# FNet mixing gated by a squared-ReLU layer, one core: a chunk's P and Q written out in two halves, and the side work of VectorE on earlier steps

## The chip, the cores and the metric

The kernel runs on one core of a Trainium2 chip. The metric is the device time of one execution in microseconds (us); lower is better. Several executions are timed and their median is compared.

## The reference, cut to what matters

```python
xn = _layernorm(x)                                    # x: 2048 x 512, over the last axis
a = einsum("bsd,ed->bse", xn, dft_hid_re)             # DFT along the hidden axis
b = einsum("bsd,ed->bse", xn, dft_hid_im)
s = einsum("ts,bse->bte", dft_seq_re, a) - einsum("ts,bse->bte", dft_seq_im, b)
h = einsum("bsd,df->bsf", xn, w1) + b1                # F = 1792
h = where(h > 0, h, 0); h = h * h
g = einsum("bsf,fd->bsd", h, w2) + b2
return x + s * silu(g)
```

All data are float32.

## The kernel before, in words

**Arithmetic.** Every float32 operand of TensorE is split into a high part, rounded by ScalarE (`split_hi`, line 136), and the rest, subtracted by VectorE (`split_lo`, line 139). Each product is three matmuls: high by high, high by low, low by high. Most products of 2 x 2 blocks go by a scheme of seven products instead of eight (`PRODUCTS`). It needs sums of blocks on both sides, which VectorE makes before the split (`sums_a_steps`, `sums_b_steps`), and sums of the seven results (`closing_of`, `combine`).

**Stages.** First come the layer norm and, with it, the products of sequence chunk 0 (`products`, line 399, with 512 columns). The two sequence transforms of xn, called P and Q, are made for eight chunks `c` of 256 rows. Chunk 0 uses plain products. Chunk 1 takes four of its eight inner steps as plain products (`MIXED`, `plain_step`) and four by the seven products; while the mixed steps run, VectorE makes the sums over xn that the scheme needs on its stationary side. Those are eight operations on 128x1024 in two groups of four inner blocks (`side[0]` and `side[1]`, made by `sums`, line 273), and after them one split for each of the eight inner blocks (`split_sums`, tile `xc`). Chunks 2 to 7 are all in the scheme: eight steps `(c, j)` of 42 matmuls (`mm`, line 388). Then follow the y units (`YUnit`, `r_A` to `r_D`, line 799), which apply the hidden transform to P and Q; the h units, which use w1; and the output products with w2 (`outer`, line 905).

**A step of a chunk.** In step n the code issues the 42 matmuls; then the sums of the DFT operand of step n+2 (`step_sums`, tile `u`, lines 300 to 303); the split of step n+1 (`step_split`: ScalarE `g<-u`, then VectorE `g<-u,g`); the load of the operand of step n+4 (`step_load`, three buffers `u`); one or two of the sums that close the chunk before (`closing`, tile `c`, made from PSUM and from copies called `left`); and last whatever the table `EARLY` names for that step. Each engine takes its instructions in this written order. There are two `g` buffers, so ScalarE can split step n+1 only once TensorE is done with step n-1.

**The closing of a chunk.** In the last step of a chunk `some(closing, 2)` starts it: ScalarE copies product 1 into tile `c`, and VectorE adds products 2 and 6. The other five sums (six for chunk 1) are spread by the tables `LATER` and `LATER_1` over steps 0 to 4 (0 to 5) of the next chunk. All chunks use one buffer, tagged `e`, for tile `c`. Its content, 1024 KB, goes to DRAM tile `pqd` in one DMA on SyncE's queue, issued at j = 5 (`max(LATER_1)`, line 660). The next chunk's first copy into tile `c` has to wait until that DMA has landed. Chunk 7 is closed after the last step, among the first y work (line 966).

**Side jobs.** `EARLY` names jobs by a letter and a number; each mention runs one piece of the job. `d0` to `d3` and `v0`, `v1`, `v6` are the weights' jobs (wd and w1): a load of the raw weight (line 438), the first sum, the other two sums, the split and DMA of three blocks, the split and DMA of four (line 451). They share two buffers tagged `pq00` and `pq01`, and `p0` to `p3` load the results back for the y units (tile `wdp`, line 499). `y0`, `y1`, `y2` are the operands of the first y units (`y_early`): a load from `pqd`, all three sums (lines 310 to 314), two splits (tile `yg`).

**SyncE's queue.** All loads of `u`, the raw weights, `wdp`, `yr` and `yraw`, and the stores to `pqd`, `wdd` and `w1d` are issued by SyncE in written order. A DMA that waits holds those behind it.

**The first y unit.** It takes product 1 (`r_A`), product 7 (`r_D`), product 6 (`r_B`), 2 (`r_A`), 5 (`r_B`), 4 (`r_C`), 3 (`r_B`). Before product 6 ScalarE must copy minus `r_A` into `r_B`; before product 3 VectorE must have read `r_B` (`c22`, line 809).

Of the kernel before, what the change touches and what calls it, by code (L numbers as in the profile page):

```python
# [34 lines left out]


EARLY = {
# [8 lines left out]
}  # L46
LATER = {0: 1, 1: 1, 2: 1, 3: 1, 4: 1}
LATER_1 = {0: 1, 1: 1, 2: 1, 3: 1, 4: 1, 5: 1}


Y_SIDE = (
# [73 lines left out]
C21, C11, C22, C12 = range(4)  # L125
# [5 lines left out]
def fnet_gated_kernel(ctx, tc, x, xt, ct, wd, w1, w2, b1, b2, out):  # L131
    nc = tc.nc
    ctx.enter_context(tc.manual_schedule(engines=None))

    def split_hi(hi, lo, src):
        nc.scalar.activation(hi, src, AF.Copy)  # L136

    def split_lo(hi, lo, src):
        nc.vector.tensor_tensor(lo, src, hi.bitcast(F32), op=ALU.subtract)  # L139

    def split(*parts):
        split_hi(*parts)
        split_lo(*parts)
# [15 lines left out]
    PQD = [dram.tile([P, 2, 4, 256], F32, name=f"pqd{c}") for c in range(NC)]  # L159
# [6 lines left out]
    def bank(tag, name):  # L166

        return acc.tile([P, 512], F32, tag=tag, name=name)
# [4 lines left out]
    def operand_buf(tag, name, step, shape=(2, 7, 256)):  # L173

        first = START.get(tag, 0)
        skip = (step - first) % 4 * LANE
        size = shape[0] * shape[1] * shape[2]
        room = ROOM.get(tag, 0)
        flat = buf(tag, [P, size + (room or skip)], name, F32R)
        a, b, c = shape  # L180
        return flat[:, skip:skip + size].rearrange("p (a b c) -> p a b c", a=a, b=b, c=c)
# [94 lines left out]
    def split_sums(j):  # L276
        s = xn32[j].rearrange("p h (b n) -> p (h b) n", b=2)
        split(XC[j][:, S2:S1 + 1, HI, :], XC[j][:, S2:S1 + 1, LO, :], s)
# [9 lines left out]
    def plain_parts(c, j, hs=slice(0, 2)):  # L288
        if (c, j) not in part:
            part[c, j] = operand_buf("g" + "ab"[j % 2], f"g{c}_{j}", 0 if c or j == NJ - 1 else 3 if j in TURNED else 1, (2, 4, CW))  # L290
        g, r = part[c, j], raw[c, j]
        s = slice(2 * hs.start, 2 * hs.stop)
        return g[:, HI, s], g[:, LO, s], r[:, s]

    def sums_b(t, r):
        list(sums_b_steps(t, r))
# [8 lines left out]
    def sums_a(*operands):  # L305
        list(sums_a_steps(*operands))

    def sums_a_steps(t, a21, a11_a22, a11, a12, turned=False):

        nc.vector.tensor_tensor(t[:, 0:2], a21.to_broadcast([P, 2, 256]), a11_a22, op=ALU.subtract)  # L310
        yield
        if turned:
            nc.vector.tensor_tensor(t[:, 2], a11, t[:, 1], op=ALU.subtract)
            nc.vector.tensor_tensor(t[:, 3], a12, t[:, 2], op=ALU.subtract)  # L314
        else:
            nc.vector.tensor_tensor(t[:, 2], t[:, 1], a11, op=ALU.subtract)
            nc.vector.tensor_tensor(t[:, 3], t[:, 2], a12, op=ALU.add)  # L317

    def sums_rows(t, r, turned=False):

        sums_a(t, r[:, C12:C12 + 1], r[:, C11:C22 + 1], r[:, C11], r[:, C21], turned)

    def sums_w1_steps(t, r):
        return sums_a_steps(t, r[:, 0:1], r[:, 1:4:2], r[:, 1], r[:, 2], True)
# [10 lines left out]
    def step_sums(n):  # L335
        if n < len(steps):
            u = raw[steps[n]]
            sums_b(u[:, 4:8], u)
# [71 lines left out]
    def plain_step(j):  # L410

        g = part.pop((1, j))
        for k, pairs_ in ((2, ((A11, 1), (A12, 3))), (4, ((A21, 1), (A22, 3))), (3, ((A11, 0), (A12, 2))),
                          (Z, ((A21, 0), (A22, 2)))):
            if k not in ms:
                ms[k] = bank("ba" if k == Z else banks(1)[k], f"m{k}_1")
            for i, (a, q) in enumerate(pairs_):
                mm(ms[k], XC[j][:, a], lambda b_: g[:, b_, q], j == MIXED[0] and not i, k == Z and j == MIXED[-1] and i == 1)
# [6 lines left out]
    def go(*names):  # L425


        for v in names:
            if v[0] == "h" and int(v[1:]) >= NTC * NP:
                continue  # L430
            if v not in making:
                making[v] = makers[v[0]](int(v[1:]))
            next(making[v])
# [46 lines left out]
    def y_early(n):  # L480

        k = n // 2
        r = buf(f"pq{k}0", [P, 4, 256], f"yr{n}")
        load_pq(n, r)
        yield
        t = buf(f"pq{k}1", [P, 4, 256], f"yt{n}")
        sums_rows(t, r, True)
        yield
        g = yop[n] = operand_buf(Y_HOME[n // 2 % 3][n % 2], f"yg{n}", 1 if n % 6 else 3)
        split(g[:, HI, 4:7], g[:, LO, 4:7], r[:, 0:3])  # L490
        yield
        split(g[:, HI, 0:4], g[:, LO, 0:4], t)
        yield
# [55 lines left out]
    side = sums(0), sums(1)  # L549
# [51 lines left out]
    def some(steps_, n):  # L601
        for _ in range(n):
            next(steps_)

    for i, j in enumerate(MIXED):
        if i == 0:
            some(side[0], 2)
            split(*plain_parts(1, MIXED[1]))
            split_sums(0)
            for k in range(ND):  # L610
                plain_out(k)
            for k in range(2):
                nc.sync.dma_start(PQD[0][:, k].rearrange("p k n -> p (k n)"), plain[k])
            some(side[1], 1)
        elif i == 1:
            split_sums(1)
            split(*plain_parts(1, MIXED[2]))
            some(side[1], 1)
            split_sums(2)
            go("d0")  # L620
        elif i == 2:
            split_sums(3)
            some(side[1], 1)
            split(*plain_parts(1, MIXED[3]))
            step_sums(0)
            go("d0", "d0")
        else:
            step_sums(1)
            some(side[1], 1)
            step_split(0)  # L630
            split_sums(4)
            split_sums(5)
        plain_step(j)
        load_c(*order[NJ + i + 4])

# [2 lines left out]
    for n, s in enumerate(steps):  # L638
        c, j = s
        if c > 1 and j == 0:  # L640
            ms = {}
        for k, tag in banks(c).items():
            if k not in ms:
                ms[k] = bank(tag, f"m{k}_{c}")
        g = part.pop(s)
        for p in FIRST if j == 0 and c > 1 else ORDER:
            a, b = PRODUCTS[p]
            mm(ms[p], XC[j][:, a], lambda b_: g[:, b_, b], j == 0 and (c > 1 or p in (1, 5, 6, 7)), s in LAST)
        step_sums(n + 2)
        step_split(n + 1)  # L650
        if n < 2:
            split_sums(6 + n)
        if n == 0:
            e = buf("e", [P, 2048], "c1")
            copy(chunk_part(e)(C22), halves(ms[Z]))
        step_load(n + 4)
        if closing:
            some(closing, (LATER_1 if c == 2 else LATER).get(j, 0))
            if j == max(LATER_1):
                nc.sync.dma_start(PQD[c - 1].rearrange("p h k n -> p (h k n)"), e)  # L660
                closing = None
        if s in LAST:
            if c > 1:
                e = buf("e", [P, 2048], f"c{c}")
            room = {}
            if c < NC - 1:
                room = buf("pq10", [P, 2, 512], f"left{c}")
                room = {7: room[:, 0], 5: room[:, 1], 3: buf("pq11", [P, 512], f"left3_{c}")}
            closing = closing_of(chunk_part(e), ms, room, c == 1)
            some(closing, 2)  # L670
        if s == (2, 4):
            nc.vector.transpose(stats_t, stats.rearrange("p m h j -> p (m h j)"))
            for q in range(4):
                nc.sync.dma_start(rows[:, q * 32:(q + 1) * 32], stats_t[q * 32:(q + 1) * 32, :])
        go(*EARLY.get(s, ()))
# [326 lines left out]
    for u in range(2, NC):  # L1002
        n = 2 * u + 2
# [41 lines left out]
    for n in range(NTC * NP):  # L1045
        unit = HUnit(n)
        first, second, later = H_SIDE.get(n, ((), (), ()))
# [39 lines left out]
    for n in range(NTC * NP):  # L1087
        c, p = divmod(n, NP)
# [37 lines left out]
        if p == NP - 1 and not last:  # L1126
            e = buf("e", [P, 4, 512], f"z{c}")
# [16 lines left out]
    e = buf("u", [P, 4, 512], f"z{c}")  # L1144
# [95 lines left out]
```

## Time and profile before

| What | Value |
|---|---|
| median of three timed runs | 676.29 us (676.1 to 677.19) |
| profiled execution: own time | 673.96 us |
| profiled execution: span | 672.1 us |
| granted TensorE clock, mean | 0.999 |
| share of the span: TensorE matmul, VectorE, ScalarE | 99%, 90%, 57% |
| DMA | 150.85 MB, mean 224 GB/s |

The profiled execution's own time stands 1.9 us above its span: that lies outside the span. PE is TensorE's matmuls and PEld its weight loads, which run beside matmuls; DVE is VectorE, ACT ScalarE, SP SyncE, SPq SyncE's queue of DMAs. In a list of waits the columns are the waiting line, the one that released it, the total in us, the number of times and the longest. In a timeline the columns are start, duration, engine, line, operation and tiles; brackets hold the engine's idle time just before and what ended it. The mean of a matmul row is its own duration; matmuls overlap.

### The profile page before, as it was taken

How to read it: one execution, taken by the hardware profiler on the slowest of the kernel's cores; microseconds unless marked ns; L12 is line 12 of the kernel's file. 1: busy time of each engine (PE TensorE's matmuls, PEld its weight loads, DVE VectorE, ACT ScalarE, POOL GpSimd, SP SyncE). 2: the span in 40 equal slices, each digit the busy share in tenths (PEclk: the TensorE clock that was granted, in tenths of full speed). 3: DMA queues.
4: the chain of work that ended last, by engine and by line, in shares of the span. 5: the costliest groups of instructions: out<-in, count | busy, mean ns of one | idle time of the engine just before them, and what ended most of it. 6: DMA issues, size and time to landing. Idle time of an engine off the chain costs nothing.

```text
span 672.1 us, 13519 instructions
## 1 busy us (share of the span) xinstructions
PE 663.7 (99%) x5605; PEld 651.5 (97%) x5605; DVE 608.0 (90%) x844; ACT 381.0 (57%) x516; POOL 8.8 (1%) x11
## 2 busy tenths in 40 slices
PE   8999999999999999999999999999999999999997
PEld 5889999999999999999899999999999999999997
DVE  7998999899989999998799988977887889999997
ACT  6855563535445454544365547788778765454451
POOL 0000000000000000000000000000000000101010
PEclk9999999999999999999999999999999999999999
DMA  8735264948659485879488668576755866677775
GB/s 284 234 105 186 87 219 145 325 138 285 238 184 352 150 282 193 280 271 319 157 298 279 201 188 299 199 262 214 267 182 196 328 241 211 179 232 194 215 204 157
DMA packets 51741, 150.85 MB, mean 224 GB/s; under 512 B 4960, under 2 KB 19552, under 8 KB 50272
## 3 DMA queue, kind: packets, MB, share of 16 engines
q1 hardware_dynamic: 43568, 129.28, 57.6%
q10 hardware_dynamic: 6208, 18.88, 7.1%
q0 software_dynamic: 1904, 1.84, 1.9%
q8 instruction: 44, 0.72, 0.4%
q14 instruction: 17, 0.14, 0.1%
HBM read 101.98 MB, written 47.99 MB: 223 GB/s over the span
## 4 chain that ended last, share of the span: by engine, by line
PE 89%; DVE 6%; DMA 2%; ACT 2%; issue 1%; SPq 0%; DVEq 0%; ACTq 0%
PE m L388 34%; PE m_o L905 15%; PE r_B L799 13%; PE r_A L799 9%; PE pq_b L399 4%; PE r_C L799 4%; PE r_D L799 4%; PE m_last L905 4%; PE pq_bb L399 1%; DMA pqd<-c 1%; DVE g L139 1%; DMA x<-in_x 1%; DVE c L373 1%; DVE xc L139 1%; DVE xn L273 1%
## 5 line engine op out<-in xcount | busy, mean ns | idle before, releaser
L388 PEld LDWEIGHTS m<-g,xc 128*128 128x128 f32 x2376 | 270.1, 188 | 0.9 <-DVE g L139 0.5
L388 PE MATMUL m<-g,xc 128*128 128x256 f32 x2376 | 270.6, 276 | 0.3 <-DVE g L139 0.3
L136 ACT ACTIVATE g<-u 128x1792 fp32r<-128x1792 f32 (+2 forms) x65 | 101.6, 1564 | 132.4 <-PE m L388 85.3
L139 DVE TENSOR_TENSOR g<-u,g 128x1792 fp32r<-128x1792 f32 (+2 forms) x66 | 120.0, 1819 | 9.1 <-ACT g L136 8.9
L905 PE MATMUL m_o<-w,g 128*128 128x256 f32 x882 | 100.5, 276 | 0.0
L905 PEld LDWEIGHTS m_o<-w,g 128*128 128x128 f32 x882 | 100.3, 188 | 0.0
L136 ACT ACTIVATE g<-hr 128x1792 fp32r<-128x1792 f32 (+2 forms) x31 | 48.2, 1565 | 40.0 <-DVE hr L317 17.8
L799 PE MATMUL r_B<-xT,w 128*128 128x256 f32 x504 | 66.5, 276 | 0.0
L799 PEld LDWEIGHTS r_B<-xT,w 128*128 128x128 f32 x504 | 61.5, 188 | 0.0
L139 DVE TENSOR_TENSOR g<-hr,g 128x1792 fp32r<-128x1792 f32 (+2 forms) x31 | 56.7, 1838 | 2.9 <-ACT g L136 2.8
L799 PE MATMUL r_A<-xT,w 128*128 128x256 f32 x336 | 43.1, 276 | 0.0
L399 PE MATMUL pq_b<-g,xc 128*128 128x512 f32 x144 | 41.2, 392 | 1.4 <-DVE small L247 1.4
L799 PEld LDWEIGHTS r_A<-xT,w 128*128 128x128 f32 x336 | 40.3, 188 | 0.2 <-DVE xT L139 0.2
L799 PE MATMUL r_B<-wdp,yg 128*128 128x256 f32 x288 | 36.0, 277 | 1.4 <-ACT r_B L146 1.2
L300 DVE TENSOR_TENSOR u<-u 128x512 f32<-128x512 f32 x52 | 35.6, 685 | 0.8 <-DMA u<-in_ct 0.7
L799 PEld LDWEIGHTS r_B<-wdp,yg 128*128 128x128 f32 x288 | 34.1, 188 | 1.8 <-ACT r_B L146 1.4
L399 PEld LDWEIGHTS pq_b<-g,xc 128*128 128x128 f32 x144 | 26.7, 188 | 8.1 <-ACT g L136 2.2
L905 PE MATMUL m_last<-w,g 128*128 128x256 f32 x294 | 33.5, 276 | 0.0
L905 PEld LDWEIGHTS m_last<-w,g 128*128 128x128 f32 x294 | 33.4, 188 | 0.0
L139 DVE TENSOR_TENSOR yg<-yraw,yg 128x1792 fp32r<-128x1792 f32 x13 | 26.2, 2018 | 0.8 <-ACT yg L136 0.8
L136 ACT ACTIVATE yg<-yraw 128x1792 fp32r<-128x1792 f32 x13 | 22.2, 1710 | 7.9 <-DVE yraw L314 7.3
L302 DVE TENSOR_TENSOR u<-u 128x256 f32<-128x256 f32 x52 | 22.1, 425 | 1.8
(185 smaller groups left out, 835.0 us busy)
## 6 DMA issues: line engine op xcount, KB each, us to landing
u<-in_ct SPq DMA_DIRECT2D x63, 512.0 KB, 3.8
hd<-h ACTq DMA_DIRECT2D x28, 512.0 KB, 5.1
hr<-hd SPq DMA_DIRECT2D x28, 512.0 KB, 3.7
pqd<-c SPq DMA_DIRECT2D x7, 1024.0 KB, 7.6
wdp<-wdd SPq DMA_DIRECT2D x8, 896.0 KB, 7.2
yraw<-pqd SPq DMA_DIRECT2D x13, 512.0 KB, 5.7
w<-w1d SPq DMA_DIRECT2D x6, 896.0 KB, 8.1
y<-y ACTq DMA_DIRECT2D x8, 512.0 KB, 4.9
```

What stands on the lines that cost most here:

```text
L136: nc.scalar.activation(hi, src, AF.Copy)
L139: nc.vector.tensor_tensor(lo, src, hi.bitcast(F32), op=ALU.subtract)
L273: nc.vector.tensor_tensor(s[:, :, to], s[:, :, a], s[:, :, b], op=op)
L300: nc.vector.tensor_tensor(t[:, 0:2], r[:, 0:1].to_broadcast([P, 2, 256]), r[:, 1:3], op=ALU.add)
L302: nc.vector.tensor_tensor(t[:, 2], t[:, 1], r[:, 1], op=ALU.add)
L373: nc.vector.tensor_tensor(part_(to), halves(room.get(m, ms[m])), part_(frm), op=op)
L388: nc.tensor.matmul(ps[:, d], w[:, a_, d * P:(d + 1) * P], halves(mv(b_)), start=first and d == 0 and (a_, b_) == (HI, HI), stop=last and ( ...
L399: nc.tensor.matmul(accs[k], w, part[0, j][:, b_, 2 * h:2 * h + 2], start=j == 0 and h == 0 and (a_, b_) == (HI, HI), stop=j == NJ - 1 and ...
L799: nc.tensor.matmul(self.region(REGION[k]), w, mv, start=i == 0 and k in (1, 7), stop=i == len(ops) - 1, skip_group_check=True)
L905: nc.tensor.matmul(m[:, i * 256:(i + 1) * 256], ready[n][:, a_, H_SLOT[a], i * P:(i + 1) * P], W2[p][:, b_, b], start=p == 0 and i == 0 an ...
```

## The change

It has four parts.

1. The store of P and Q: half `[:, 0]` of a chunk's tile `c` is issued at j = 3 of the next chunk and half `[:, 1]` at j = 4, 512 KB each, where one DMA of 1024 KB stood at j = 5. For chunk 1 `LATER_1` puts two sums on j = 1, so that its six are done by j = 4.
2. The sums over xn: the last four stand in the first two mixed steps instead of all four mixed steps; the splits of these sums move up with them.
3. `EARLY`: the pieces of the weights' jobs stand on earlier steps. `v6` ends at (5, 6) instead of (6, 4), and `p0` is loaded at (6, 1) and (6, 6) instead of (6, 6) and (7, 0).
4. `y_early` runs its three sums in two pieces, as the weights' jobs do.

```diff
 EARLY = {
-    (1, 2): ("d0", "d1"), (2, 0): ("d0",), (2, 1): ("d1",), (2, 3): ("d1",), (2, 4): ("d1", "d2"), (2, 6): ("d1",),
...
+    (1, 1): ("d0", "d1"), (1, 2): ("d0",), (2, 0): ("d1",), (2, 2): ("d1",), (2, 3): ("d1", "d2"), (2, 5): ("d1", "d2"),
...
-LATER_1 = {0: 1, 1: 1, 2: 1, 3: 1, 4: 1, 5: 1}
+LATER_1 = {0: 1, 1: 2, 2: 1, 3: 1, 4: 1}
...
-        sums_rows(t, r, True)
+        first = sums_rows_steps(t, r, True)
+        next(first)
+        yield
+        list(first)
...
         if i == 0:
             some(side[0], 2)
+            some(side[1], 2)
             split(*plain_parts(1, MIXED[1]))
             split_sums(0)
+            split_sums(1)
...
+        elif i == 1:
             some(side[1], 1)
-        elif i == 1:
-            split_sums(1)
             split(*plain_parts(1, MIXED[2]))
+            split_sums(2)
+            split_sums(3)
             some(side[1], 1)
-            split_sums(2)
             go("d0")
         elif i == 2:
-            split_sums(3)
-            some(side[1], 1)
+            step_sums(0)
             split(*plain_parts(1, MIXED[3]))
-            step_sums(0)
             go("d0", "d0")
+            split_sums(4)
         else:
             step_sums(1)
-            some(side[1], 1)
             step_split(0)
-            split_sums(4)
             split_sums(5)
+            split_sums(6)
...
-        if n < 2:
-            split_sums(6 + n)
+        if n == 0:
+            split_sums(7)
...
-            if j == max(LATER_1):
-                nc.sync.dma_start(PQD[c - 1].rearrange("p h k n -> p (h k n)"), e)
+            if j in (3, 4):
+                q = slice((j - 3) * 1024, (j - 2) * 1024)
+                nc.sync.dma_start(PQD[c - 1][:, j - 3].rearrange("p k n -> p (k n)"), e[:, q])
+            if j == 4:
                 closing = None
```

SyncE's queue over steps (7, 3) to (7, 5), in the program before. `u7_7` is the last DFT operand, `pqd6` the store of chunk 6, `wdp2` the two loads of p2.

```order
L286 DMA u7_7_3455<-in_ct 128x1024
L458 DMA yr0_3460<-pqd0_75 128x1024
L499 DMA wdp2_3462<-wdd2_85 128x1792
L458 DMA yraw3_3512<-pqd1_76 128x1024
L458 DMA yr2_3515<-pqd1_76 128x1024
L499 DMA wdp2_3462<-wdd2_85 128x1792
L458 DMA yraw4_3566<-pqd2_77 128x1024
L660 DMA pqd6_81<-c6_3231 128x2048
```

The same stretch of the queue in the changed program:

```order
L285 DMA u7_7_3460<-in_ct 128x1024
L665 DMA pqd6_81<-c6_3237 128x1024
L459 DMA yr0_3466<-pqd0_75 128x1024
L503 DMA wdp2_3468<-wdd2_85 128x1792
L459 DMA yraw3_3518<-pqd1_76 128x1024
L665 DMA pqd6_81<-c6_3237 128x1024
L459 DMA yr2_3522<-pqd1_76 128x1024
L503 DMA wdp2_3468<-wdd2_85 128x1792
L459 DMA yraw4_3573<-pqd2_77 128x1024
```

The store, which came last, now stands as two, each right behind the load of its step and ahead of `yr` and `wdp2`.

VectorE in the last mixed step and the first step of the scheme, before. `u_2` and `g_1` are the sums of step 2 and the split of step 1; `xc_122` to `xc_124` are the splits of sums 4 to 6.

```order
L303 TENSOR_TENSOR u_1_680<-u_1_680 128x256
L273 TENSOR_TENSOR xn_4_374<-xn_4_374 128x4x256
L139 TENSOR_TENSOR g_0_750<-u_0_620,g_0_750 128x1792
L139 TENSOR_TENSOR xc_122<-xn_4_374,xc_122 128x4x256
L139 TENSOR_TENSOR xc_123<-xn_4_374,xc_123 128x4x256
L300 TENSOR_TENSOR u_2_744<-u_2_744 128x512
L302 TENSOR_TENSOR u_2_744<-u_2_744 128x256
L303 TENSOR_TENSOR u_2_744<-u_2_744 128x256
L139 TENSOR_TENSOR g_1_856<-u_1_680,g_1_856 128x1792
L139 TENSOR_TENSOR xc_124<-xn_4_374,xc_124 128x4x256
```

The same place in the changed program:

```order
L302 TENSOR_TENSOR u_1_684<-u_1_684 128x256
L138 TENSOR_TENSOR g_0_752<-u_0_623,g_0_752 128x1792
L138 TENSOR_TENSOR xc_123<-xn_4_374,xc_123 128x4x256
L138 TENSOR_TENSOR xc_124<-xn_4_374,xc_124 128x4x256
L299 TENSOR_TENSOR u_2_747<-u_2_747 128x512
L301 TENSOR_TENSOR u_2_747<-u_2_747 128x256
L302 TENSOR_TENSOR u_2_747<-u_2_747 128x256
L138 TENSOR_TENSOR g_1_858<-u_1_684,g_1_858 128x1792
L138 TENSOR_TENSOR xc_125<-xn_4_374,xc_125 128x4x256
```

The sum over xn ahead of `g_0` is gone from here, and the splits stand one inner block further on.

VectorE in step (2, 5) of the changed program, with the end of step (2, 4):

```order
L374 TENSOR_TENSOR c_863<-m_1_584,c_863 128x2x256
L678 STREAM_TRANSPOSE stats_t<-stats 128x32
L299 TENSOR_TENSOR u_7_1248<-u_7_1248 128x512
L301 TENSOR_TENSOR u_7_1248<-u_7_1248 128x256
L302 TENSOR_TENSOR u_7_1248<-u_7_1248 128x256
L138 TENSOR_TENSOR g_6_1360<-u_6_1195,g_6_1360 128x1792
L138 TENSOR_TENSOR wd1g<-wd1t,wd1g 128x1024
L299 TENSOR_TENSOR wd2t<-wd2r 128x512
L299 TENSOR_TENSOR u_0_1306<-u_0_1306 128x512
```

Two pieces of weights' jobs, the last split of `d1` and the first sum of `d2`, now stand between two steps' sums; the last sum of the closing of chunk 1 has moved from this step to the one before.

More of the change, by code (lines that the diff above doesn't have):

```diff
@@ L317, in sums_a_steps, with sums_rows_steps, sums_rows @@
             nc.vector.tensor_tensor(t[:, 3], t[:, 2], a12, op=ALU.add)
-    def sums_rows(t, r, turned=False):
-        sums_a(t, r[:, C12:C12 + 1], r[:, C11:C22 + 1], r[:, C11], r[:, C21], turned)
+    def sums_rows_steps(t, r, turned=False):
+        return sums_a_steps(t, r[:, C12:C12 + 1], r[:, C11:C22 + 1], r[:, C11], r[:, C21], turned)
+    def sums_rows(*operands):
+        list(sums_rows_steps(*operands))
     def sums_w1_steps(t, r):
```

13 rows, old and new, of the table EARLY are left out of this document.

## The prediction

> **What bounds the kernel now.** I read the page's engine lines first, then busy time by stage, then the waits of TensorE's weight loads, then the timeline where those waits lie.
>
> ```profile
> span 672.1 us, 13519 instructions
> PE 663.7 (99%) x5605; PEld 651.5 (97%) x5605; DVE 608.0 (90%) x844; ACT 381.0 (57%) x516; POOL 8.8 (1%) x11
> ```
>
> TensorE is busy almost throughout, and the change neither adds nor removes a matmul. A gain can only be idle time of TensorE. By stage (start and end, length, busy time of PE, PEld, DVE):
>
> ```profile
> 78.10:322.30 244.20, 243.89 (x2144) 243.43 (x2143) 228.14 (x286) 116.61 (x98) 0.00 (x0) 1.00 0.69 239
> 322.30:333.90 11.60, 10.18 (x85) 9.69 (x85) 11.09 (x17) 4.76 (x8) 0.00 (x0) 1.00 0.19 66
> 655.00:672.10 17.10, 13.08 (x116) 12.88 (x114) 12.33 (x23) 3.32 (x7) 1.21 (x1) 0.95 0.58 154
> ```
>
> The second row, the first y units, loses most among the stages that the change touches. The last row, the kernel's end, loses more, but nothing there is changed. The weight loads' waits name the places:
>
> ```profile
> PEld r_B L799 <- ACT r_B L146: 1.4, 1, 1.4
> PEld m L388 <- DVE g L139: 0.5, 1, 0.5
> PEld r_B L799 <- DVE y L809: 0.4, 1, 0.4
> PEld m L388 <- ACT c L146: 0.2, 1, 0.2
> ```
>
> The first and third are the y stage's. Its timeline shows their cause:
>
> ```profile
> 307.66 0.68 DVE L373 TENSOR_TENSOR c<-m,c 128x512 f32<-128x512 f32 x1
> 312.47 0.44 SPq L660 DMA_DIRECT2D pqd<-c  x1
> 321.75 0.60 ACT L146 ACTIVATE c<-m 128x512 f32<-128x512 f32 x1 [6.03 <-DMA pqd<-c]
> 322.39 1.29 DVE L373 TENSOR_TENSOR c<-m,c 128x512 f32<-128x512 f32 x2 [4.41 <-ACT c L146]
> 322.41 1.67 PE L799 MATMUL r_A<-wdp,yg 128*128 128x256 f32 x12
> 323.91 1.52 PE L799 MATMUL r_D<-wdp,yg 128*128 128x256 f32 x12
> 325.23 1.06 ACT L136 ACTIVATE yg<-yt 128x1024 fp32r<-128x1024 f32 x1 [2.14 <-DVE yt L314]
> 326.19 0.37 ACT L146 ACTIVATE r_B<-r_A 128x256 f32<-128x256 f32 x1
> 326.61 1.63 PE L799 MATMUL r_B<-wdp,yg 128*128 128x256 f32 x12 [1.18 <-ACT r_B L146]
> 328.98 3.20 DVE L373 TENSOR_TENSOR c<-m,c 128x512 f32<-128x512 f32 x5
> 329.44 1.52 PE L799 MATMUL r_B<-wdp,yg 128*128 128x256 f32 x12
> 330.80 1.52 PE L799 MATMUL r_C<-wdp,yg 128*128 128x256 f32 x12
> 332.57 1.65 PE L799 MATMUL r_B<-wdp,yg 128*128 128x256 f32 x12 [0.25 <-DVE y L809]
> ```
>
> The store of chunk 6 is issued at 312.47. ScalarE's first copy of chunk 7 waits for its landing until 321.75. VectorE sits idle 4.41 us behind that copy, so the sums of y2 come late, ScalarE's split of them comes late, and behind it in ScalarE's queue the copy that seeds `r_B` ends at 326.56. TensorE waits for that. VectorE then does the other closing sums until 332.18, and the read of `r_B` that stands behind them makes the second wait.
>
> Twelve matmuls take 1.36 us (329.44 to 330.80). So `r_B` could have started at 323.91 + 1.36 = 325.27 and was 1.34 late; the last row could have started at 332.16 and was 0.41 late. Matmuls overlap, so PE's bracket is 0.16 short in both cases. This is where a rule matters: the Trainium skill, in "Perfetto Trace Analysis", section "Identifying the Most-Contended Engine", says that matmul busy time is a poor measure, since matmuls are pipelined, and that the weight loads' busy share should be used. The trace agrees: the weight loads' waits at these two places (1.4 and 0.4) are nearer to the spacing than the matmul rows' brackets. By the matmul brackets the whole sum would be 1.74 us and the forecast 674.6; by the weight loads' four waits, 2.5 and 673.8. I use the spacing.
>
> **The change part by part.** *Mixed steps.*
>
> ```profile
> 51.62 26.81 PE L388 MATMUL m<-g,xc 128*128 128x256 f32 x235
> 51.82 1.06 ACT L136 ACTIVATE g<-u 128x1024 fp32r<-128x1024 f32 x1 [4.54 <-PE pq_b L399]
> 52.91 1.23 DVE L139 TENSOR_TENSOR g<-u,g 128x1024 fp32r<-128x1024 f32 x1 [1.98 <-ACT g L136]
> 69.80 1.22 DVE L273 TENSOR_TENSOR xn<-xn 128x1024 f32<-128x1024 f32 x1
> 73.64 1.71 ACT L136 ACTIVATE g<-u 128x1792 fp32r<-128x1792 f32 x1 [0.57 <-ACT xc L136]
> 76.67 2.02 DVE L139 TENSOR_TENSOR g<-u,g 128x1792 fp32r<-128x1792 f32 x1
> 78.74 13.48 PE L388 MATMUL m<-g,xc 128*128 128x256 f32 x115 [0.31 <-DVE g L139]
> ```
>
> The split of step (1, 1) ends at 78.69 and TensorE starts at 78.74; by the bracket plus 0.16 it lost 0.47. VectorE had been behind since the mixed steps, although it stood idle 1.98 us before 52.91: it waited for ScalarE's split, which waited for a buffer that TensorE held (51.82). Two sums over xn, 1.22 each by the row at 69.80, now stand in that gap: 1.98 us of idle become work. Ahead of the split of (1, 1) one xc split of about 1.2 us is added (same 128x1024 size). Net, VectorE reaches that split some 0.8 us earlier, at about 75.9, still after ScalarE's part (75.35), and ends at 77.9. TensorE wants it at 78.27. The stall goes: -0.47. Its bounds are 0 and -0.5. The splits needed by the mixed steps themselves move later by the two sums' excess over the gap, about 0.5 us; TensorE wants the first only at the second mixed step, 48 matmuls or 5.4 us after 51.62, and it ends near 54.6.
>
> *Store in halves.* The last closing sum of chunk 6 ends at 308.34 and its half can be issued then, 4.1 us before 312.47; the other half goes a step (4.76 us, 42 matmuls) earlier. What matters is the second landing. How long such DMAs take, in us from issue to landing:
>
> ```profile
> pqd<-plain SPq DMA_DIRECT2D x2, 512.0 KB, 3.2
> pqd<-c SPq DMA_DIRECT2D x1, 1024.0 KB, 9.2
> wdp<-wdd SPq DMA_DIRECT2D x1, 896.0 KB, 9.3
> ```
>
> The first is two halves of chunk 0's store in a quiet place; the second is the store at 312.47; the third the load of p2 issued at 308.62, the slowest near by. So the second half lands between 311.6 and 317.7. The old landing, 321.7, led to `r_B` at 326.6, 4.9 us later; for 325.27 a landing by 320.3 is enough, and for the second wait as well (1.34 + 0.41 earlier) one by 319.9. Both ends lie before that. The copy then has only product 1 of chunk 7's last step to wait for: that step starts 4.76 before 322.41, so about 318.4. That is 3.3 earlier than 321.75, more than the 1.75 needed. So -1.34 and -0.41, bounds 0 and -1.75. At the start of chunk 3 the same wait costs the weight load 0.2 and the matmuls less; I take -0.1 (0 to -0.2). In the other chunks the copy's wait is hidden by TensorE's 42 matmuls and is worth nothing. Six more DMA issues cost SyncE 0.44 us each (312.47); that hurts only if a load behind them is late, which the next part prices.
>
> *Weights' jobs and y sums in two pieces.* The same instructions, so nothing by itself; the cover is VectorE's spare time per step, and the price is paid where too much falls on one step.
>
> ```profile
> 84.33 0.68 DVE L300 TENSOR_TENSOR u<-u 128x512 f32<-128x512 f32 x1
> 85.85 2.02 DVE L139 TENSOR_TENSOR g<-u,g 128x1792 fp32r<-128x1792 f32 x1
> 87.79 0.95 DVE L139 TENSOR_TENSOR wd0g<-wd0r,wd0g 128x768 fp32r<-128x768 f32 x1
> 125.68 1.22 DVE L139 TENSOR_TENSOR wd1g<-wd1t,wd1g 128x1024 fp32r<-128x1024 f32 x1
> 127.25 0.69 DVE L300 TENSOR_TENSOR u<-u 128x512 f32<-128x512 f32 x1 [0.35 <-DMA u<-in_ct]
> 308.31 1.71 ACT L136 ACTIVATE g<-u 128x1792 fp32r<-128x1792 f32 x1 [3.05 <-PE m L388]
> 310.05 2.02 DVE L139 TENSOR_TENSOR g<-u,g 128x1792 fp32r<-128x1792 f32 x1 [0.18 <-ACT g L136]
> ```
>
> A step's own work on VectorE is 84.33 to 87.79, 3.46 us, which leaves 1.30 of 4.76. A split that starts as soon as ScalarE allows (310.05) ends at 312.07; TensorE takes it at about 312.8 (two steps before 322.4), so VectorE may be 0.7 late. The fullest steps of the new table are (2, 5) and (4, 5) with a four-block split and a first sum (1.22 + 0.69 = 1.91), (3, 2) and (5, 2) with that split and a closing sum (1.90), (3, 5) and (5, 5) with two sums and a three-block split (about 1.8). Each is at most 0.61 over 1.30, under 0.7, and the next step is light. The old table had such pairs too, at (2, 0) and (3, 4), and in the list above `m` waited for VectorE's `g` once only, at 78.74. I take 0; above, 0.26 a step if a load also comes 0.35 late as at 127.25 (0.61 + 0.35 - 0.7), six steps, +1.6; below, 0, because no TensorE wait is left there to win.
>
> Sum: -0.47 - 0.10 - 1.34 - 0.41 = -2.32. The profiled execution had 673.96 us around its span of 672.1, so 671.6; the median of the runs, 676.29, stands 2.3 above it, and I carry the difference over: 676.29 - 2.32 = 674.0.
>
> **The rivals.** *Crowded steps cost something.* Late operands at some of the six steps take back 0.5 to 1.6 us: 674.5 to 675.6. For it speaks the wait at 127.25; against it, that the store then in flight, 1024 KB in one, is now two halves a step apart.
>
> *The load of p2 replaces the store.* Its second half now stands behind both half stores. It landed 9.3 after 308.62, at 317.9. Two halves ahead of it, at 3.2 us each, add 6.4 at most, to 324.3, and less because part of the old store moved beside it too. TensorE needs it from the seventh matmul of `r_A` on, at 323.1. A landing at 324.1 costs 1.0: 675.0.
>
> *The halves land no earlier.* Then only the mixed steps gain: 676.29 - 0.47 = 675.8. It decides at a landing after 321.7, 13 us after issue, where the rows show at most 9.3. The Trainium skill speaks for this rival: "DMA: Bandwidth & Descriptors", section "Bandwidth", advises DMAs of at least 1 MiB for three quarters of the peak rate. The trace does not bear it out at this size: 3.2 us for half the bytes.
>
> *Slower.* Loads of `u` queue behind a weight's store, the next raw weight and a half store, all issued within a step, and VectorE starts the sums of the six full steps late. To end at 677.64 (0.2% slower) it must lose 2.32 + 1.35 = 3.67, or 0.61 a step: every operand 0.7 late (0.09 of room is left). The trace has twice that distance between its worst case, 0.35 once, and this.
>
> **How the numbers follow.** Forecast 0.63; crowded steps 0.14; load of p2 0.07; halves no earlier 0.07; slower 0.07; 0.02 for what I did not see. Changes below 0.2%, 1.35 us, cannot be told from none. Faster than 674.94 are the forecast, half of the crowded steps and some of the p2 case: 0.72. The same: the rest of these and the halves, 0.20. Slower 0.08. The floor is 676.29 less the larger bound, 2.5, and 0.4 for the runs' own spread: 673.4. The range goes up to the halves' case, 675.8, and leaves out the slower one.
>
> **What would show it.** Right: no wait of ScalarE's `c` for `pqd` anywhere, TensorE's rows from `r_A` to the third `r_B` of the first y unit 1.36 apart, no wait at the start of step (1, 1), the span near 669.8. Wrong: a new wait of `m` for VectorE's `g` one step after (2, 5), (3, 2), (4, 5) or (5, 2), or `r_A` waiting for `wdp`. Above all I would be wrong if VectorE's lateness adds up over a chunk where I took each full step alone.

## The result, and the profile after

The changed kernel ran in 670.37 us (median of five, 669.75 to 670.98) beside 676.26 us for the kernel before: a ratio of 0.9924, 95% interval 0.9900 to 0.9947. Twice more, on two chips of the comparisons below, the ratio was 0.9942 (0.9921 to 0.9962) and 0.9939 (0.9926 to 0.9951). The direction was forecast. The size was not: 2.3 us were forecast, 3.6 to 5.9 were measured, and the first result lies 3 us below the range. The profiled execution took 669.75 us, 4.2 less than the profiled one of before.

The first lines of the page after:

```profile
span 668.0 us, 13540 instructions
PE 662.3 (99%) x5605; PEld 651.1 (97%) x5605; DVE 608.4 (91%) x844; ACT 381.8 (57%) x516; POOL 8.8 (1%) x11
```

Busy times are nearly those of before (PE 1.4 us less); the span fell because idle time went. The busy time by stage, over the stretches that answer to the first two rows of before:

```profile
77.40:320.20 242.80, 242.80 (x2144) 242.80 (x2144) 229.16 (x290) 117.41 (x98) 0.00 (x0) 1.00 0.71 242
320.20:331.80 11.60, 11.60 (x105) 11.60 (x104) 10.79 (x17) 4.70 (x9) 0.00 (x0) 1.00 0.39 129
```

Weight loads fill both stretches. The same 2144 matmuls took 242.8 us instead of 244.2, and 105 matmuls instead of 85 fall into 11.6 us of y units. Of the four waits of weight loads that the prediction listed none is left in the list of waits; from the mixed steps on it holds one line, which the old list had too:

```profile
PEld r_A L805 <- DVE xT L138: 0.2, 1, 0.2
```

The end of chunk 7 and the first y unit:

```profile
306.35 0.47 SPq L665 DMA_DIRECT2D pqd<-c  x1
316.44 0.60 ACT L145 ACTIVATE c<-m 128x512 f32<-128x512 f32 x1 [2.73 <-PE m L389]
317.17 1.31 DVE L374 TENSOR_TENSOR c<-m,c 128x512 f32<-128x512 f32 x2 [1.22 <-ACT c L145]
320.32 1.52 PE L805 MATMUL r_A<-wdp,yg 128*128 128x256 f32 x12
321.68 1.52 PE L805 MATMUL r_D<-wdp,yg 128*128 128x256 f32 x12
321.88 0.37 ACT L145 ACTIVATE r_B<-r_A 128x256 f32<-128x256 f32 x1 [0.77 <-PE r_A L805]
323.04 1.52 PE L805 MATMUL r_B<-wdp,yg 128*128 128x256 f32 x12
327.39 0.42 DVE L815 TENSOR_TENSOR y<-r_B,y 128x256 f32<-128x256 f32 x1 [0.38 <-PE r_B L805]
328.48 1.52 PE L805 MATMUL r_B<-wdp,yg 128*128 128x256 f32 x12
```

The half at 306.35 is the second one of chunk 6. From issue to landing it took, in us:

```profile
pqd<-c SPq DMA_DIRECT2D x1, 512.0 KB, 8.0
```

So it landed at 314.35, where the one store of before, 9.2 us on the way, had landed at 321.7. Of these 7.3 us, 6.1 come from the earlier issue and only 1.2 from a shorter way. ScalarE's copy into `c` now waits for TensorE's product, not for the store. The seed of `r_B` waits for `r_A`, its own input, and rows stand 1.36 us apart. In the mixed steps the split of step (1, 1), which had ended at 78.69, ends at 77.10, and TensorE's first row runs on past it (192 matmuls of the mixed steps, 42 of step (1, 0) and more):

```profile
51.02 29.19 PE L389 MATMUL m<-g,xc 128*128 128x256 f32 x256
75.08 2.02 DVE L138 TENSOR_TENSOR g<-u,g 128x1792 fp32r<-128x1792 f32 x1
```

### The profile page after: what moved, and what is told of

It is laid out like the page before. It is cut to its first block, busy times and chain, and to the rows that moved or that the text cites. A ratio compares the mean times of both kernels' runs of the same rounds, so it can differ in the third digit from the quotient of the medians.

```text
span 668.0 us, 13540 instructions
## 1 busy us (share of the span) xinstructions
PE 662.3 (99%) x5605; PEld 651.1 (97%) x5605; DVE 608.4 (91%) x844; ACT 381.8 (57%) x516; POOL 8.8 (1%) x11
## 4 chain that ended last, share of the span: by engine, by line
PE 97%; DVE 2%; DMA 0%; issue 0%; ACT 0%; DVEq 0%; ACTq 0%
PE m L389 40%; PE m_o L911 15%; PE r_B L805 13%; PE r_A L805 9%; PE pq_b L400 5%; PE r_C L805 4%; PE r_D L805 4%; PE m_last L911 4%; PE pq_bb L400 2%; DVE z L1161 0%; DVE z L961 0%; DMA x<-in_x 0%; DVE z L966 0%; ACT z L957 0%; DVE m_last L1178 0%
```

## Experiments

All compare with the kernel before on the same chip. "Lost time" is worked out from each trace: over all matmul starts from the first mixed step to the closing stage, the spacing beyond 113.3 ns, summed. What is left of a profiled execution's own time without it is 669.1 to 670.3 us in all fourteen profiles. If the start of the first mixed step (50.97 to 52.21 us, in code that all kernels share) is taken off too, 617.9 to 618.1 are left. So these profiles differ by their start-up and by TensorE's waits and what follows them, and by little else. About 0.7 us of each lost time lies behind the first y units, at the same places in every profile.

| Kernel | median us | ratio to before (95%) | profiled us | lost time us |
|---|---|---|---|---|
| before | 676.26 | 1 | 673.96 | 4.32 |
| after | 670.37 | 0.9924 (0.9900 to 0.9947) | 669.75 | 0.68 |
| e1 before again | 675.15 | 0.9994 (0.9976 to 1.0012) | 674.17 | 4.95 |
| e2 halves only | 672.91 | 0.9960 (0.9941 to 0.9978) | 672.79 | 3.38 |
| e3 mixed steps only | 674.33 | 0.9986 (0.9968 to 1.0005) | 673.94 | 4.56 |
| e4 jobs' table only | 678.77 | 1.0039 (1.0021 to 1.0057) | 678.12 | 8.06 |
| e5 after again | 671.30 | 0.9942 (0.9921 to 0.9962) | 670.75 | 1.38 |
| e6 after, store at j = 5 | 677.56 | 1.0031 (1.0014 to 1.0048) | 677.57 | 8.01 |
| e7 after, one store at j = 4 | 670.82 | 0.9931 (0.9912 to 0.9951) | 671.41 | 2.30 |
| e8 after, old table | 672.06 | 0.9950 (0.9933 to 0.9967) | 672.59 | 2.33 |
| e9 after with waits put in | 680.66 | 1.0072 (1.0059 to 1.0086) | 680.66 | 11.26 |
| e10 after, old mixed steps | 672.93 | 0.9964 (0.9951 to 0.9977) | 672.86 | 2.92 |
| e11 after, y1 later | 670.81 | 0.9933 (0.9919 to 0.9946) | 669.80 | 0.69 |
| e12 after a third time | 671.50 | 0.9939 (0.9926 to 0.9951) | 672.67 | 2.89 |

Chips: e1 to e4 one, e5 to e8 another, e9 to e12 a third. The kernel before had a median of 675.04 us there on the first (35 runs), 674.94 on the second (17) and 675.68 on the third (11); the differences below are from these.

**e1, the kernel before again** (no edit).

> The kernel before, once more. Theory 'exposed landings': its timed runs are slower than its profiled execution because TensorE's waits at the chunk starts and at the first y unit hang on when a 1024 KB store lands, which differs from run to run; then a second profile shows the same four places with other sizes (y unit between 1 and 4 us in all), and the timed runs spread over 2 us or more. Rival 'profiling offset': the same waits to within 0.1 us (0.47 at step (1, 1), 1.34 and 0.41 at the y unit) and timed runs near 676 again.

Its weight loads' waits:

```profile
PEld r_B L799 <- ACT r_B L146: 1.4, 1, 1.4
PEld m L388 <- DVE g L139: 0.5, 1, 0.5
PEld r_B L799 <- DVE y L809: 0.4, 1, 0.4
PEld m L388 <- ACT c L146: 0.3, 1, 0.3
```

The same four to 0.1 us: in these two executions the waits hardly vary, as the rival said. Yet the timed runs spread from 673.5 to 678.1, and at chunk 3's start the two profiles lost 0.67 and 1.22 us. There the spacing of matmul starts shows two waits, 0.13 and 0.08 us in the first profile, 0.31 and 0.08 in the second. Behind the second wait 124 matmuls of the second profile stood about 0.118 us apart, and 42 of the first; I call this the slow pace. It makes 0.37 of the difference and the longer wait 0.18, so what varies most there is what follows a wait.

**e2, the halves alone.** The store's edit and `LATER_1` from the diff above, nothing else.

> Only the store in halves (and LATER_1). Theory 'a stall costs more than its wait': after a wait the second matmul comes 0.22 instead of 0.113 us later and up to 40 matmuls stand 0.118 apart, so chunk 3's start gives 0.74 and the y unit 2.1: span 2.8 us under the old one with the stall at step (1, 1) still there. Rival (my sum): waits alone, 0.1 + 1.75 = 1.85 us. By the theory of exposed landings the median falls by 4 to 5 us and the spread of the timed runs shrinks to about 1 us; by the offset rival the median falls by 2 to 3.

The median fell by 2.1 and the timed runs lay within 1.8 us. The waits for the store are gone, but the slow pace took part of the gain back. Behind 0.13 us of wait at step (2, 3) came 292 matmuls at the slow pace (with the restart's two spacings 294, seven whole steps), 1.54 us in all. Two stretches of 16 us, one in it and one behind it:

```profile
110.00:126.00 16.00, 16.00 (x138) 16.00 (x138) 14.43 (x19) 6.79 (x5) 0.00 (x0) 1.00 0.70 221
144.00:160.00 16.00, 16.00 (x143) 16.00 (x143) 15.33 (x19) 7.72 (x7) 0.00 (x0) 1.00 0.73 242
```

TensorE is busy in both, the granted clock is 1.00 in both, and five matmuls fewer pass in the first.

**e3, the mixed steps alone.** The order of the mixed steps and of `split_sums`, nothing else.

> Only the mixed steps' new order. Theory: the stall at step (1, 1) goes and takes 0.47 + 0.11 + 0.17 = 0.74 us with it; the waits for the store stay, so the median falls by 0.7 and the spread of the timed runs stays that of the kernel before. Rival (my sum): 0.47.

0.7 us less by the median, as the theory said, but the interval takes in 0.47 and none at all. The stall at (1, 1) is gone from the trace; those for the store stand, and the last of them now has 149 matmuls at the slow pace behind it, which is why this profile's lost time is no less than that of before.

**e4, the table alone.** `EARLY` and the y sums in two pieces; the store stays at j = 5.

> Only the weights' jobs on earlier steps and the y sums in two pieces, with the old store and the old LATER_1. Step (2, 5) then holds a four-block split, a first sum and a closing sum, 1.14 + 0.61 + 0.60 = 2.35 us by start-to-start times, 1.05 over the 1.30 that a step has to spare and 0.35 over the room. Theory 'room': one new wait of TensorE of about 0.35 us at step (2, 7), 0.5 to 0.6 us with its slow restart, and otherwise no change: 0 to +0.6 us. Rival 'the jobs themselves matter': moving the stores and loads away from the store of P and Q lets it land earlier, and the waits for it shrink by 1 us or more.

Neither alone: 3.7 us slower. The wait that 'room' forecast at step (2, 7) is there, 0.40 us by the spacing and 0.53 in all, and one like it at (1, 3), 0.91 in all; ahead of neither does VectorE wait for `u`, so these are its own work. But the larger losses, 1.18 at (4, 1) and 1.56 at (6, 1), stand behind late loads. At the start of chunk 6, SyncE's queue and VectorE's row:

```profile
238.79 0.42 SPq L664 DMA_DIRECT2D pqd<-c  x1
240.07 0.53 SPq L452 DMA_DIRECT2D w1d<-w16g  x1
240.65 1.64 SPq L459 DMA_DIRECT2D yr<-pqd  x1
243.53 0.33 SPq L285 DMA_DIRECT2D u<-in_ct  x1
251.17 0.69 DVE L299 TENSOR_TENSOR u<-u 128x512 f32<-128x512 f32 x1 [1.88 <-DMA u<-in_ct]
```

The store of P and Q, a store of v6 and the load of y1 stand ahead of the load of `u`, which lands 7.6 us after its issue. VectorE waits 1.88 us, TensorE 1.25 at the start of (6, 1). In the list of waits:

```profile
PEld m L389 <- DVE g L138: 3.1, 5, 1.3
DVE u L299 <- DMA u<-in_ct: 4.1, 5, 1.9
```

**e5, the changed kernel again** (no edit).

> The changed kernel once more. Theory 'no stall, no slow pace': its profile again shows 0.113 us between matmuls from the mixed steps to the y units, and its timed runs lie within about 1.5 us of each other. Rival 'luck': a wait of 0.1 us or more somewhere between 50 and 430 us in this execution, and a spread like that of the kernel before (3 us or more).

Partly luck. At the same place, the start of (6, 1), this execution waited:

```profile
246.13 0.69 DVE L299 TENSOR_TENSOR u<-u 128x512 f32<-128x512 f32 x1 [1.03 <-DMA u<-in_ct]
PEld m L389 <- DVE g L138: 0.4, 1, 0.4
```

In the first profile after, VectorE's wait there had been 0.4, and TensorE had not felt it. The timed runs spread over 3.1 us, because of one at 673.67.

**e6, the store at j = 5 again.** In the changed kernel:

```diff
-            if j in (3, 4):
-                q = slice((j - 3) * 1024, (j - 2) * 1024)
-                nc.sync.dma_start(PQD[c - 1][:, j - 3].rearrange("p k n -> p (k n)"), e[:, q])
-            if j == 4:
+            if j == 5:
+                nc.sync.dma_start(PQD[c - 1].rearrange("p h k n -> p (h k n)"), e)
```

> The changed kernel with one store of 1024 KB at j = 5, as before, and the rest of the change kept. My own sum (the store is worth 1.85, the rest 0.47): about 2 us slower than the changed kernel. Theory 'the halves make room for the weights' jobs': the store at j = 5 meets the four-block and three-block stores of (3, 5), (4, 5), (5, 5) in the queue, loads of u take 7 us, VectorE waits 1 us or more for them at the starts of chunks 4 and 6, and the kernel is 5 to 8 us slower than the changed one, slower than the kernel before.

6.3 us slower than the changed kernel of the same comparison, and slower than before. Both kinds of wait are there:

```profile
PEld m L389 <- DVE g L138: 2.7, 4, 1.5
DVE u L299 <- DMA u<-in_ct: 6.8, 7, 2.1
ACT c L145 <- DMA pqd<-c: 7.3, 2, 6.2
```

**e7, one store at j = 4.** As e6, with `j == 4`.

> The changed kernel with the store in one piece of 1024 KB at j = 4. If the second landing alone counts (the 'earlier' theory), it is as fast as the changed kernel within 0.3 us. If the size counts (the 'smaller' theory), loads of u issued beside it land late again, with a wait of VectorE for u of 0.3 us or more and some of TensorE: 1 us or more slower.

Within 0.5 us of the changed kernel, so the earlier issue carries the gain and the halving is not shown to add any. The store of chunk 6, 1024 KB issued at 308.11, took 8.2 us to land here, beside the 8.0 of the second half of 512 KB in the first profile after. The waits that the size theory named are there too, in this one execution (VectorE for `u` 4.1 us, TensorE 0.8); the medians do not tell the two apart:

```profile
PEld m L389 <- DVE g L138: 0.8, 2, 0.5
DVE u L299 <- DMA u<-in_ct: 4.1, 5, 1.1
```

**e8, the old table in the changed kernel.** `EARLY` and `y_early` as before.

> The changed kernel with the old table of side jobs. The run with the halves alone had a wait of 0.13 us at step (2, 2), where the doubled closing sums of (2, 1) meet d1's first sum (0.60 + 0.60 + 0.61 over 1.30), and 294 matmuls at the slow pace behind it. Theory 'room': the same wait here, 0.1 to 0.3 us plus 0.1 to 1.4 us of slow pace, nothing else, since the store no longer meets the jobs: 0.3 to 1.7 us slower than the changed kernel. Rival 'the table is worth nothing': the same time as the changed kernel within 0.3 us.

0.8 us slower by the medians, which is not clear of noise: the runs, 671.70 to 672.59, lie within those of e5, 670.58 to 673.67. The wait of e2 returned at the same step, (2, 3) (the expectation calls it (2, 2)), with the same 292 slow matmuls and 1.54 us lost. With the store early the new table saves at most about that; with the store late it costs 3.7 (e4) and 3 (e6 beside e3, by the ratios).

**e9, waits put in.** In the changed kernel, after `go(*EARLY...)`:

```diff
+AGAIN = {(2, 4): 2, (3, 4): 2, (4, 4): 2, (5, 4): 3, (6, 4): 3, (7, 2): 3}
...
+        for _ in range(AGAIN.get(s, 0)):
+            u = raw[steps[n + 2]]
+            nc.vector.tensor_tensor(u[:, 4:6], u[:, 0:1].to_broadcast([P, 2, 256]), u[:, 1:3], op=ALU.add)
```

> The changed kernel with six waits put in: after steps (2, 4), (3, 4), (4, 4) VectorE repeats the first sum of an operand twice, after (5, 4), (6, 4), (7, 2) three times (0.7 us each, same values). ScalarE's split then starts late and TensorE should wait at the start of the second step after: some 0.2 to 0.4 us at the first three places and about 1.1 us at the others, 4 us in all. Theory 'slow pace': behind each wait the second matmul comes 0.22 us later, and between 2 and 300 matmuls stand 0.118 instead of 0.113 apart, their number different from place to place and run to run; cost 0.1 to 1.4 us a place beyond the wait, 5 to 8 us in all, and timed runs spread over 2 us or more. Rival 'a wait costs itself': 0.113 from the third matmul on everywhere, 4 to 4.7 us in all, spread as in the changed kernel (1.3 us).

Of the weight loads' waits:

```profile
PEld m L390 <- DVE g L139: 7.3, 11, 1.4
```

There were eleven waits, not six: VectorE was late for two steps running at four of the six places, and one wait, at (6, 1), is that of e5. So the sizes I had given were too small. 9.2 us were lost by the medians. In the trace 10.6 were lost, beyond the 0.7 that every profile has, to 7.3 us of wait. The pace behind the waits varied as expected: at six of them it was back at 113 ns within six matmuls, at the other five it stayed slow for some 40 to 166, or until the next wait. The spread of the timed runs was 2.5 us beside 2.0 for the changed kernel on that chip, which decides nothing. That a wait costs more than itself is shown; that it makes the timed runs spread is not.

**e10, the old mixed steps in the changed kernel.**

> The changed kernel with the old order of the mixed steps. Theory: the stall at step (1, 1) returns (0.47 + 0.11, and slow pace of 0.1 to 1.4 us), and since d0's first split now stands a step earlier, VectorE is late once more at step (1, 3), as in the run with the table alone (0.25 us there): 0.8 to 2.5 us slower than the changed kernel. Rival (my sum): 0.47 us slower, one wait only.

1.4 us slower by the medians. The stall at (1, 1) came back, and so did the second wait that I had expected, at (1, 3): only 0.06 us by the spacing, too short for the list of waits, and each with slow matmuls behind it, 1.3 us in all. Two starts late by about 0.1 us elsewhere lost another 0.9 with their slow pace; VectorE had waited for late `u` in that part of the trace. The two profiles themselves do not show a gain: 2.92 us lost here, 2.89 in e12.

**e11, y1 later.** In the changed kernel's `EARLY`:

```diff
-(5, 5): ("v6", "v6", "y1"), (5, 6): ("v6",),
-(6, 0): ("y1",), (6, 1): ("y1", "p0"), (6, 6): ("p0",),
+(5, 5): ("v6", "v6"), (5, 6): ("v6",),
+(6, 0): ("y1",), (6, 1): ("p0",), (6, 2): ("y1",), (6, 3): ("y1",), (6, 6): ("p0",),
```

> The changed kernel with y1's load moved from (5, 5) to (6, 0) and its sums to (6, 2) and (6, 3). In three of four profiles with the new table, u landed 6 to 7 us after its issue at (5, 6), beside two stores of v6 and this load, and TensorE waited at the start of (6, 1). Theory 'crowded queue': without the 512 KB load u lands 1 us or more earlier, no wait of TensorE at (6, 1), and the median is 0.3 to 0.7 us below the changed kernel's on this chip. Rival 'crowded VectorE': the wait stays, same time.

The load of `u` issued at (5, 6), in us from issue to landing, first in e11 and then in e5:

```profile
u<-in_ct SPq DMA_DIRECT2D x1, 512.0 KB, 4.6
```

```profile
u<-in_ct SPq DMA_DIRECT2D x1, 512.0 KB, 6.8
```

It landed 2.2 us earlier, VectorE waited for no `u`, and TensorE for nothing from the mixed steps to the y units. In the three profiles of the changed kernel (first, e5, e12) this load took 6.2, 6.8 and 7.1 us, and VectorE waited 0.4, 1.0 and 1.4 for it. The median is 0.7 us below that of e12 beside it, but their runs overlap (669.80 to 672.54 and 670.67 to 672.67). The wait's cause is shown; the gain is not clear of noise.

**e12, the changed kernel a third time** (no edit).

> The changed kernel a third time, to stand beside the other three on this chip. By both theories 670 to 671.5; by the crowded-queue theory a wait at the start of (6, 1) of 0 to 0.5 us, with 0.1 to 1.4 us of slow pace behind it where it occurs.

The wait at (6, 1) was there, 0.76 us this time, and one at (7, 5), also behind a late `u`:

```profile
PEld m L389 <- DVE g L138: 1.1, 2, 0.8
```

## Why the prediction was right and wrong

*The places.* Right. Every wait that was to go went. The copy's wait for `pqd` is gone from the list. The second half landed at 314.35, inside the forecast's 311.6 to 317.7, and the rival in which the halves land no earlier fell. But the reason that I gave against that rival was wrong: I set 3.2 us, from a quiet place, against 9.2 at a crowded one. At the crowded place the half took 8.0, and it landed early because it was issued early.

*The price of a wait.* This is the step that failed. I took a wait to cost its bracket plus 0.16 us. The term for step (1, 1), forecast at 0.47, was 0.76 in the trace of before; chunk 3's start, 0.10, was 0.67; the two y waits, 1.34 and 0.41, were 1.45 and 0.54; and a small one ahead of `r_A`, 0.21, I left out. Together 3.63, not 2.32. That is the gain in lost time between the two profiles (4.32 - 0.68 = 3.64). With it the forecast would have been 672.7, below the range that I gave. This is 1.3 of the 3.6 us by which the forecast missed the first result. The missing part stood in rows that I quoted: 326.61 to 329.44 is 2.83 us for twenty-four matmuls, and I had measured 1.36 for twelve elsewhere. My bracket plus 0.16 gave the wait itself rightly (0.47, 1.34 and 0.41 by the spacing). What I left out is what follows it: behind each wait the second matmul starts 0.22 us after the first, and often the pace stays at about 0.118 us for a while (e2, e9). For chunk 3 I also halved the weight load's 0.2 on no ground, and saw one wait where there are two.

*From a profile to the median.* I carried one execution's sum over to the median unchanged: the median of before stood 2.3 above its profile, and I took that to stay. That of after stands 0.6 above its own, which makes 1.7 of the miss. The two first profiles differ by 4.2 us and the first medians by 5.9. 0.6 of the 4.2, the rest of the miss, lies ahead of the mixed steps, in code that both share: the first `m` started at 51.62 and at 51.02. In the two later comparisons the medians differ by 3.6 and 4.2, near the 3.64 of lost time. The later 63 runs of before spread from 673.4 to 680.7, and their medians lie 0.6 to 1.3 below the 676.26 of the first five, so part of the first 5.9 is the draw or the chip; which was not found. Nor was why the first three timed runs of before lay 2.3 above their profile; e1 shows two executions whose waits are nearly the same and whose stretches behind them are not.

*The table.* I priced it at nothing, by VectorE's room per step. In the changed kernel that is nearly right: 0 to 2 us of lost time from execution to execution, at (6, 1) and (7, 5), which is the forecast's rival of crowded steps, though not at the steps that I had listed as fullest. But there the steps are decided by loads that land late and not by VectorE's own work (e11). In e4, where the same table meets the late store, I expected at most 0.6 us and 3.7 were lost: 1.4 at two steps by VectorE's own work, which the new mixed steps and `LATER_1` relieve (neither wait stands in e6), and most of the rest behind late loads.

*The parts are not a sum.* The store moved early without the table is worth 2.9 us beside its own before (e8, with the new mixed steps), the table alone costs 3.7 (e4), and both together gain 3.6 to 4.2 (e5, e12). In e4 and e6 the store at j = 5 stands beside the jobs' stores and loads of j = 5 and 6, and loads of `u` land late behind them.

*The rivals.* The load of p2 did not take the store's place: `r_A` stands on time. The slower case did not come, but e4 and e6 show its mechanism where the store had not moved, at nearly the price that I gave it in all, though at a few steps and not at all six.

## What to carry to other kernels

Price a wait of TensorE by the spacing of matmul starts until the old pace is back, not by the bracket in front of one row. Before a list of side jobs is moved, look at what stands in the DMA queue ahead of the next operand's load at the new place: here the same table cost 3 to 3.7 us where one store was issued late, and nothing that is clear of noise where it was issued early. One profile of each kernel is one draw, even where the waits look steady.

## What the runs showed of the hardware

After a wait TensorE can run at about 118 ns a matmul instead of 113.3 with no further wait and a granted clock of 1.00, for up to 292 matmuls; the stretch in e2 cost more (about 1.3 us) than the wait ahead of it (0.13). The longer stretches behind a wait in the chunks mostly held 40, 124, 166 or 292 matmuls. With the restart's two spacings these are one, three, four and seven whole steps of 42, so the pace seems to come back where a step begins. The restart itself, 0.22 us to the second matmul, was there behind nearly every wait. But a wait is not needed: in all fourteen profiles some 38 matmuls of the h units (from 392.97 us on in the first profile after) stand about 0.118 us apart with no wait ahead of them, 0.18 us in all. What starts and ends the slow pace was not settled.

The time from issue to landing of the same DMA goes with what stands beside it: one load of `u`, 512 KB, took 4.6 us without the load of y1 ahead of it (e11), 6.2 to 7.1 with it (the changed kernel) and 7.6 with the store of P and Q ahead of it as well (e4).
